# Two row tiles of x loaded from ScalarE's queue, the keys' weight second in SyncE's queue

## The chip, the cores and the metric

One core of a Trainium2 chip. The metric is the device time of one execution, in microseconds (us), lower is better. TensorE (PE) multiplies matrices, VectorE (DVE) and ScalarE (ACT) work elementwise, GpSimd (POOL) builds masks, and SyncE (SP) issues most transfers. ScalarE can issue transfers too, from a queue of its own. Both queues' transfers are carried by the core's 16 transfer engines.

## The reference

x has 2048 rows of 512, in bf16. Two blocks follow one another, each behind a layer norm without weights:

```python
h  = x + _A_ref(_layernorm(x), A_wqkv, A_wo)      # linear attention, 32 heads of 16
h2 = h + _B_ref(_layernorm(h), B_w1, B_w2)        # relu(.. @ w1) @ w2, inner width 1792

phi = lambda t: jnp.where(t > 0, t + 1, jnp.exp(t)) + 1e-6
pq, pk = phi(q), phi(k)
kv = einsum("bhsd,bhse->bhde", pk, v);  z = sum of pk over the rows
o  = (pq @ kv) / (pq . z + 1e-6)                  # then @ wo
```

## The kernel before

The rows are cut into 16 tiles of 128, and the tiles into four chunks of 512 rows. The order of all work is written out by hand: the string `ORDER` is a list of words, and each word calls the function `op_` of its name with the numbers behind it. The words are issued one after the other, each to the engine that its function names, so an engine works through its own words in the order of the string. Waits between engines and for transfers are put in for the data that a word reads and writes.

The words that matter here, t being a tile:

- `lx.t.n` loads n tiles of x from tile t on, issued by SP (line 219). `ax.t.n` does the same from ScalarE (line 222); the kernel before has the function and does not call it. `lk`, `lq`, `lv`, `lo`, `l1`, `l2` load weights (line 225); `lk` loads the keys' weight `wk_sb`, 512 KB.
- `table` loads the table of ScalarE's functions (line 183). `warm.n.b.w` issues n matmuls on zeros (line 250), ahead of the first real work of PE.
- `S.t` and `A.t` are the two steps of mean and variance of a tile of x (lines 253 and 254, VectorE). `R.t` makes 1/sqrt(var + eps) with a Ln and an Exp (lines 259 and 260, ScalarE). `N.t` normalises into `h_nat` (line 267, VectorE).
- `T.t` transposes the normalised tile on PE (line 292), `E.t` copies it out of PSUM on ScalarE (line 302). From tile 5 on most tiles are transposed by a transfer instead (`X.t`, line 313).
- `K.t` multiplies tile t by the keys' weight (line 321), `Q` projects queries (line 329), `G` accumulates (line 373). `F`, `U`, `M`, `D` make phi of the keys.
- In the second half `h.t` multiplies by the folded output weight (line 501), `hD.t` adds x on VectorE and so empties its bank (line 507), `s.t`, `a.t`, `n.t` are the second layer norm on VectorE (lines 255, 256, 275), `x.t` its transpose by transfer (line 314). `p` and `f` are the two matmuls of the feed-forward block (lines 516 and 545), `pD` and `fo` their evictions on VectorE (lines 536 and 553), and `fd` stores.

In the kernel before, all loads go through SP: tile 0, tile 1, tile 2, the keys' weight, tile 3, tiles 4 and 5, tiles 6 and 7, the queries' weight, and then four tiles at a time. On PE the first real words are T.0, T.1, T.2, K.0, K.1, T.3, K.2, K.3.

The table of the order is one string; no other function differs between the kernels.

Of the kernel before, what the change touches and what calls it, by code (L numbers as in the profile page):

```python
# [15 lines left out]


ORDER = """
table const lx.0.1 warm.66.7.64 lx.1.1 masks lx.2.1 lk.0.4 lx.3.1 S.0 lx.4.2 S.1 lx.6.2 lq.0.4 A.0 A.1 S.2 R.0.1
warm.2.7 lx.8.4 R.1.1 N.0 lx.12.4 A.2 N.1 T.0.1 R.2.1 T.1.6 E.0 N.2 E.1 T.2.4 S.3 K.0.2 E.2 A.3 S.4 K.1.4.2.2 R.3.1  # L20
K.1.4.0.2 F.0.1 N.3 A.4 U.0.1 S.5 T.3.5 K.2.6.2.2 E.3 S.7 K.2.6.0.2 F.1.1 K.3.3.0.2 M.0.1 A.5 U.1.1 D.0.1 K.3.3.2.2
M.1.1 R.4.2 Q.0.3.1 S.6 F.3.1 A.7 A.6 N.5 F.2.1 Q.0.1.5 N.4 X.5 R.6.2 D.1.1 T.4.7 U.3.1 M.2.1 Q.0.0.4 M.3.1 S.8 E.4
lo.0.2 U.2.1 S.10 Q.0.2.0 qF.0.0.2 N.6 K.4.2 N.7 X.6 A.10 A.8 qU.0.0.2 S.9 K.5.3 D.3.1 X.7 A.9 D.2.1 R.8.2 G.0 S.15
F.4.2 N.8 G.1 S.13 X.8 U.4.2 S.14 G.3 qU.0.2.2 A.13 S.12 lv.0.2 G.2 M.4.2 A.12 N.9 K.7.3 R.12.2 A.15 D.4.2 X.9
qF.0.2.2 K.6.2 N.12 A.14 S.11 R.14.2 X.12 K.8.0 F.6.2 N.15 N.14 G.4 A.11 N.13 U.6.2 M.6.2 X.13 qM.0.0.2 K.9.1 R.10.2
qD.0.0.2 K.12.2 X.15 D.6.2 U.8.2 za.4.1 G.5 F.8.2 X.14 K.13.3 N.11 N.10 za.6.0 G.6 X.11 U.12.2 G.7 M.8.2 F.12.2 X.10
qM.0.2.2 K.14.0 D.8.2 M.12.2 K.15.1 lv.2.2 za.8.0 l1.0.2 K.11.3 l1.2.2 F.14.2 D.12.2 K.10.2 zf U.14.2 qD.0.2.2 G.9 zhi
F.10.2 M.14.2 G.13 zlo U.10.2 G.8 M.10.2 D.14.2 G.12 D.10.2 z.0.0 z.2.0 z.3.0 z.1.0 G.15 zc zh d4.0.2 G.11 dl4.0 dx4.0
G.14 wb.0 G.10 lo.2.2 Q.1.1.1 gA.2.2 gD.0.2 rb.0.4 Q.1.0.0 ab.0.1 rb.0.6 ab.0.3 kv.1.7 rb.0.2 kv.3.7 ab.0.7 kv.0.7
rb.0.0 kv.2.7 ab.0.5 Q.1.3.3 l2.7.7 kx qF.1.0.2 Q.1.2.2 qU.1.0.2 qM.1.0.2 m.0.4 m.2.6 m.1.5 qF.1.2.2 qD.1.0.2 m.3.7  # L30
Q.2.0.0 mD.0.2 mA.2.2 Q.2.1.1 qU.1.2.2 dm.0.0.2 Q.2.3.7 dm.0.2.2 qF.2.0.2 h.1.6 qM.1.2.2 qD.1.2.2 qU.2.0.2 h.0.2 hD.1
d4.1.4 s.1 Q.3.1.5 a.1 hD.0 nA.1 h.3.0 s.0 dl4.1 x.1 h.2.2 a.0 hD.3 nA.0 Q.2.2.6 s.3 dx4.1 x.0 Q.3.2.0 a.3 hD.2
qF.2.2.2 n.3 wb.1 Q.3.3.1 s.2 qU.2.2.2 x.3 Q.3.0.4 a.2 n.2 qF.3.2.2 qM.2.0.2 x.2 qM.2.2.2 ph.0.3.3.0 qU.3.2.2 qD.2.2.2
ph.0.0.6.0 ph.0.1.7.0 qM.3.2.2 rb.1.7 qU.3.0.2 ph.0.2.2.0 qD.3.2.2 rb.1.3 ph.0.11.1.0 rb.1.5 qD.2.0.2 ph.0.10.0.0
qF.3.0.2 rb.1.6 ph.0.10.0.1 rb.1.1 ph.0.11.1.1 rb.1.0 p.0.5.4 pD.0.10.2 rb.1.4 rb.1.2 ph.0.2.2.1 ph.0.3.3.1 l2.0.7
qM.3.0.2 ph.0.0.6.1 pD.0.2.2 p.0.6.0 ph.0.1.7.1 qD.3.0.2 p.0.4.3 pD.0.0.2 p.0.7.1 pA.0.4.2 dm.1.2.2 d4.2.5.2 dm.1.0.2
p.0.8.2 dl4.2 pD.0.6.2 dl4.3 p.0.9.3 dx4.2 p.0.13.5 dx4.3 pD.0.8.2 wb.2 r.0.4 h.4.7 h.6.0 hD.4 rb.2.3 f.3.1.0.7 rb.2.1
s.4 rb.2.0 a.4 rb.2.6 rb.2.2 p.0.12.4 rb.2.5 rb.2.7 h.7.2 pD.0.12.2 rb.2.4 f.3.1.7.7 wb.3 hD.7 s.7 h.5.4 hD.6
f.2.3.7.7 hD.5 f.1.6.0.7 dm.2.2.2 dm.2.0.2 s.6 rb.3.2 h.8.0 rb.3.7 a.6 s.5 f.1.6.7.7 rb.3.0 hD.8 rb.3.5 rb.3.6 n.4 s.8
rb.3.3 f.2.3.0.7 a.5 rb.3.1 fo.1 rb.3.4 n.5 a.7 x.5 h.9.7 n.7 n.6 fo.2 f.0.0.7.7 x.4 fo.3 dm.3.2.2 h.10.5 x.7 dm.3.0.2  # L40
h.11.6 hD.9 x.6 hD.10 h.13.3 s.10 h.15.2 fd.3.0.2 fd.3.2.2 a.10 a.8 n.10 hD.11 h.14.7 x.10 s.11 f.0.0.0.7 n.8 a.11
hD.15 s.9 p.1.3.5 hD.13 p.1.8.2 hD.14 fo.0 p.1.2.4 s.15 h.12.1 s.14 p.1.9.3 s.13 a.13 p.1.7.7 pD.1.8.2 p.1.6.6 a.9
n.11 r.8.4 n.13 p.1.12.0 n.9 r.4.4 a.14 a.15 x.9 n.14 p.1.11.3 hD.12 pD.1.2.2 p.1.13.1 x.11 p.1.10.2 n.15 pD.1.6.2 x.8
p.1.0.5 pD.1.10.2 p.1.5.4 fd.1.0.2 fd.1.2.2 x.14 p.1.1.6 s.12 pD.1.12.2 f.5.2.7.7 fd.2.0.2 fd.2.2.2 fd.0.0.2 fd.0.2.2
x.15 pD.1.0.2 p.1.4.3 p.2.2.5 pD.1.4.2 f.5.2.0.7 p.2.6.3 fo.5 p.2.7.4 p.2.3.6 pD.2.6.2 p.2.10.1 a.12 n.12 r.12.4
p.2.4.4 pD.2.2.2 x.12 f.7.0.0.7 fd.5.0.2 fd.5.2.2 x.13 f.7.0.7.7 p.2.5.5 fo.7 p.2.11.2 pD.2.4.2 p.2.12.3 pD.2.10.2
p.2.13.4 f.4.6.0.7 pD.2.12.2 p.2.0.5 p.3.2.1 p.3.3.2 f.4.6.7.7 f.6.0.0.7 fo.4 pD.3.2.2 p.3.9.7 p.3.8.6 f.6.0.7.7
pD.3.8.2 p.2.9.1 fo.6 p.2.1.6 fd.6 p.3.1.3 p.3.0.2 p.2.8.0 pD.3.0.2 p.3.11.4 pD.2.0.2 p.3.10.3 pD.2.8.2 p.3.5.2
# [550 lines left out]
```

## Time and profile before

| | |
|---|---|
| median of 3 runs | 168.88 us (168.74 to 168.93) |
| profiled execution | 168.48 us, span 166.8 us |
| PE | busy 162.6 us, 98% of the span |
| VectorE | busy 115.9 us, 69% |
| ScalarE | busy 49.5 us, 30% |
| HBM read, written | 9.96 MB, 2.62 MB |
| mean granted TensorE clock | 0.999 |

The profiled execution is one execution; its span runs from the first instruction to the last, and its own time lies 1.68 us above the span. Times in the views count from the span's start. In a timeline, a row gives the start, the length, the engine, the line, what is written from what, how many instructions are merged, and in brackets how long the engine had been idle before and what ended it. "SPq" and "ACTq" are the transfer issues of SyncE and ScalarE: the length is that of the issue, not of the transfer.

### The profile page before, as it was taken

How to read it: one execution, taken by the hardware profiler on the slowest of the kernel's cores; microseconds unless marked ns; L12 is line 12 of the kernel's file. 1: busy time of each engine (PE TensorE's matmuls, PEld its weight loads, DVE VectorE, ACT ScalarE, POOL GpSimd, SP SyncE). 2: the span in 40 equal slices, each digit the busy share in tenths (PEclk: the TensorE clock that was granted, in tenths of full speed). 3: DMA queues.
4: the chain of work that ended last, by engine and by line, in shares of the span. 5: the costliest groups of instructions: out<-in, count | busy, mean ns of one | idle time of the engine just before them, and what ended most of it. 6: DMA issues, size and time to landing. Idle time of an engine off the chain costs nothing.

```text
span 166.8 us, 2421 instructions
## 1 busy us (share of the span) xinstructions
PE 162.6 (98%) x920; PEld 79.8 (48%) x920; DVE 115.9 (69%) x215; ACT 49.5 (30%) x83; POOL 4.8 (3%) x21
## 2 busy tenths in 40 slices
PE   7999999999999999999999999999999999999993
PEld 7544444454544774444444444444444444464442
DVE  3899999942599979668999899564535484400532
ACT  3899996715777916200000020010000000000000
POOL 7400000000000000000000000000000000000000
PEclk9999999999999999999999999999999999999999
DMA  4975555763752446231352035312000000020122
GB/s 113 346 300 126 125 97 103 276 253 96 170 177 51 111 135 210 72 94 56 111 109 69 0 63 93 100 30 64 0 0 4 31 0 0 7 97 2 44 95 73
DMA packets 26811, 16.28 MB, mean 98 GB/s; under 512 B 16176, under 2 KB 25776, under 8 KB 26800
## 3 DMA queue, kind: packets, MB, share of 16 engines
q1 hardware_dynamic: 26336, 15.84, 33.9%
q10 hardware_dynamic: 464, 0.30, 0.7%
q8 instruction: 7, 0.11, 0.3%
q14 instruction: 4, 0.03, 0.1%
HBM read 9.96 MB, written 2.62 MB: 75 GB/s over the span
## 4 chain that ended last, share of the span: by engine, by line
PE 94%; DVE 2%; DMA 1%; ACT 0%; issue 0%
PE bk L545 29%; PE bk L516 26%; PE bk L321 8%; PE bk L373 8%; PE bk L329 8%; PE bk L501 8%; PE bk L525 3%; DMA x_nat<-in_A_x_dram 1%; DVE st L253 1%; PE bk L445 1%; DVE gT L553 1%; PE bk L397 1%; PE bk L292 1%; PE bk L419 1%; PE bk L431 1%; DVE h_nat L267 0%
## 5 line engine op out<-in xcount | busy, mean ns | idle before, releaser
L545 PE MATMUL bk<-w_sb,at 128*128 128x512 bf16 (+2 forms) x252 | 50.9, 355 | 0.0
L516 PE MATMUL bk<-lnT,w_sb 128*128 128x512 bf16 x200 | 45.6, 379 | 0.0
L536 DVE TENSOR_SCALAR at<-bk 128x1024 bf16<-128x1024 f32 x27 | 32.4, 1220 | 13.6 <-PE bk L516 10.6
L545 PEld LDWEIGHTS <-at 128*128 128x128 bf16 x252 | 23.5, 98 | 25.2 <-DVE at L536 0.3
L516 PEld LDWEIGHTS <-w_sb 128*128 128x128 bf16 x200 | 19.5, 98 | 23.1 <-issue 0.4
L553 DVE SCALAR_TENSOR_TENSOR gT<-bk,rstd,h_nat 128x512 bf16<-128x512 f32 (+2 forms) x18 | 12.1, 688 | 22.6 <-PE bk L545 20.2
L339 ACT ACTIVATE eb<-bk 128x1024 bf16<-128x1024 f32 (+1 forms) x18 | 16.6, 930 | 3.5 <-PE bk L419 1.6
L259 ACT ACTIVATE rstd<-mv,eps 128x2 f32<-128x2 f32 (+2 forms) x14 | 4.1, 294 | 44.4 <-DVE mv L256 41.6
L342 ACT ACTIVATE rb<-bk 128x1024 bf16<-128x1024 f32 (+1 forms) x18 | 16.6, 936 | 0.9 <-PE bk L321 0.9
L501 PE MATMUL bk<-m_sb,pqs 128*128 128x512 bf16 x64 | 15.3, 379 | 0.0
L321 PE MATMUL bk<-wk_sb,lnT 128*128 128x512 bf16 x64 | 15.1, 379 | 0.0
L329 PE MATMUL bk<-lnT,wq_sb 128*128 128x512 bf16 x64 | 15.0, 379 | 0.0
L373 PE MATMUL bk<-at,h_nat 128*128 128x512 bf16 x56 | 13.2, 379 | 0.0
L253 DVE BATCH_NORM_STATS2 st<-x_nat 128x6 f32<-128x512 bf16 x16 | 10.5, 675 | 1.9 <-DMA x_nat<-in_A_x_dram 1.9
L507 DVE TENSOR_TENSOR h_nat<-bk,x_nat 128x512 bf16<-128x512 f32 x16 | 10.7, 679 | 0.9 <-PE bk L501 0.8
L255 DVE BATCH_NORM_STATS2 st<-h_nat 128x6 f32<-128x512 bf16 x16 | 10.8, 687 | 0.2
L501 PEld LDWEIGHTS <-pqs 128*128 128x128 bf16 x64 | 6.3, 98 | 7.6
L373 PEld LDWEIGHTS <-h_nat 128*128 128x128 bf16 x64 | 6.1, 98 | 7.3 <-issue 0.2
L321 PEld LDWEIGHTS <-lnT 128*128 128x128 bf16 x64 | 6.0, 97 | 7.4 <-ACT lnT L302 0.3
L329 PEld LDWEIGHTS <-wq_sb 128*128 128x128 bf16 x64 | 6.1, 98 | 7.1 <-issue 0.2
L346 DVE TENSOR_SCALAR eb<-eb 128x1024 bf16<-128x1024 bf16 (+1 forms) x18 | 6.7, 389 | 0.3 <-ACT eb L339 0.3
L267 DVE TENSOR_SCALAR h_nat<-x_nat,mv,rstd 128x512 bf16<-128x512 bf16 x16 | 6.1, 400 | 0.3 <-ACT rstd L260 0.3
(62 smaller groups left out, 90.8 us busy)
## 6 DMA issues: line engine op xcount, KB each, us to landing
w_sb<-in_B_w_dram SPq DMA_DIRECT2D x4, 896.0 KB, 5.0
rr<-scr SPq DMA_DIRECT2D x28, 64.0 KB, 2.6
out_dram<-gT SPq DMA_DIRECT2D x10, 128.0 KB, 1.9
x_nat<-in_A_x_dram SPq DMA_DIRECT2D x2, 512.0 KB, 7.1
out_dram<-gT SPq DMA_DIRECT2D x11, 64.0 KB, 1.6
x_nat<-in_A_x_dram SPq DMA_DIRECT2D x4, 128.0 KB, 2.2
wk_sb<-in_A_wqkv_dram SPq DMA_DIRECT2D x1, 512.0 KB, 4.2
x_nat<-in_A_x_dram SPq DMA_DIRECT2D x2, 256.0 KB, 4.5
```

What stands on the lines that cost most here:

```text
L253: op_S = lambda t: nc.vector.bn_stats(out=st[:, t, :], in_=x_nat[:, t, :])
L255: op_s = lambda t: nc.vector.bn_stats(out=st2[:, t, :], in_=h_nat[:, t, :])
L321: nc.tensor.matmul(bk[:, b, :], lhsT=lnT[c][:, kd, j * P : (j + 1) * P], rhs=wk_sb[:, kd, :], **part(("k", t), KD),)
L329: nc.tensor.matmul(bk[:, b, :], lhsT=wq_sb[:, kd, j * P : (j + 1) * P], rhs=lnT[c][:, kd, :], start=(kd == 0), stop=(kd == KD - 1),)
L339: nc.scalar.activation(out=buf(eb, kind, i, n), in_=bank(at_bank[kind, i], n), func=ACT.Exp)
L342: nc.scalar.activation(out=buf(rb, kind, i, n), in_=bank(at_bank[kind, i], n), func=ACT.Relu)
L373: nc.tensor.matmul(bk[:, KD + kd, :], lhsT=ln_nat[:, t, kd * P : (kd + 1) * P], rhs=pk(t)[:, 0, :], start=(not stated), stop=(len(stated) ...
L501: nc.tensor.matmul(bk[:, b, :], lhsT=pqs[:, (c * KD + jb) % NQ, j * P : (j + 1) * P], rhs=m_sb[:, jb, :], start=(jb == 0), stop=(jb == KD ...
L516: nc.tensor.matmul(bk[:, b, :], lhsT=w1_sb[:, kd, f * P : (f + 1) * P], rhs=lnT[c][:, kd, :], start=(kd == 0), stop=(kd == KD - 1),)
L536: nc.vector.tensor_scalar(out=acts[c % 2][:, f : f + n, :], in0=bank(at_bank["p", c, f], n), scalar1=-1.0, scalar2=0.0, op0=ALU.mult, op1= ...
L545: nc.tensor.matmul(bk[:, b, 0 : w * P], lhsT=acts[c % 2][:, f, j * P : (j + 1) * P], rhs=w2_sb[:, f, k * P : (k + w) * P], **part(("f", t, ...
L553: nc.vector.scalar_tensor_tensor(out=o_t[:, t % NO, cols], in0=bk[:, at_bank["f", t, k], 0 : w * P], scalar=rstd2[:, t : t + 1], in1=h_nat ...
```

## The change

Tiles 1 and 2 of x are loaded with `ax` by ScalarE, ahead of its table load; so SP issues the keys' weight directly behind tile 0. The first words of `ORDER`:

```diff
-table const lx.0.1 warm.66.7.64 lx.1.1 masks lx.2.1 lk.0.4 lx.3.1 S.0 lx.4.2 S.1 lx.6.2 lq.0.4 A.0 A.1 S.2 R.0.1
+ax.1.1 const lx.0.1 warm.66.7.64 ax.2.1 lk.0.4 masks table lx.3.1 lx.4.2 lx.6.2 S.0 lq.0.4 lx.8.4 S.1 lx.12.4 A.0 A.1
...
```

The functions called are these, as they stand in both kernels:

```python
def op_lx(t, n):
    nc.sync.dma_start(out=x_nat[:, t : t + n, :], in_=rows_of(xf, t, n))

def op_ax(t, n):
    nc.scalar.dma_start(out=x_nat[:, t : t + n, :], in_=rows_of(xf, t, n))
```

SyncE at the program's start, before. `x_nat` is x in SBUF, `wk_sb` the keys' and `wq_sb` the queries' weight:

```order
L594 UNCONDITIONAL_BRANCH
L219 DMA x_nat<-in_A_x_dram 128x512 x3
L225 DMA wk_sb<-in_A_wqkv_dram 128x4x512
L219 DMA x_nat<-in_A_x_dram 128x512
L219 DMA x_nat<-in_A_x_dram 128x1024 x2
L225 DMA wq_sb<-in_A_wqkv_dram 128x4x512
```

The same place after the change:

```order
L594 UNCONDITIONAL_BRANCH
L219 DMA x_nat<-in_A_x_dram 128x512
L225 DMA wk_sb<-in_A_wqkv_dram 128x4x512
L219 DMA x_nat<-in_A_x_dram 128x512
L219 DMA x_nat<-in_A_x_dram 128x1024 x2
L225 DMA wq_sb<-in_A_wqkv_dram 128x4x512
```

Two of the three single tiles ahead of the keys' weight are gone from SP's queue; all behind them keeps its order and moves up by two places.

They stand on ScalarE now. Its start, as the difference of the two orders:

```order
 L594 UNCONDITIONAL_BRANCH
+L222 DMA x_nat<-in_A_x_dram 128x512 x2
 L183 ACT_TABLE_LOAD
 L259 ACTIVATE rstd<-mv,eps_77 128x1
```

Two issues have come in front of the table load and of all of ScalarE's activations. The orders of PE and of GpSimd are the same as before, and that of VectorE is the same up to the second half.

There VectorE moves two steps of the second layer norm, between the evictions of the feed-forward block (`at` is its inner activation, `gT` holds the output tiles):

```order
 L507 TENSOR_TENSOR h_nat<-bk,x_nat 128x512
-L255 BN_STATS st_106<-h_nat 128x6
+L255 BN_STATS st_106<-h_nat 128x6 x2
 L507 TENSOR_TENSOR h_nat<-bk,x_nat 128x512 x2
 L553 SCALAR_TENSOR_TENSOR gT<-bk,rstd_108,h_nat 128x512
-L255 BN_STATS st_106<-h_nat 128x6 x3
+L255 BN_STATS st_106<-h_nat 128x6 x2
 L256 BN_AGGR mv_107<-st_106 128x2
 L536 TENSOR_SCALAR at_101<-bk 128x1024
```

The statistics of tile 15 (s.15) stand ahead of the evictions hD.13 and hD.14 and of the output eviction fo.0. A little later n.14 moves behind s.12, past hD.12, n.15 and three evictions `pD`. In `ORDER` many other words change their places beside words of other engines, which moves nothing on any one engine.

More of the change, by code (lines that the diff above doesn't have):

```diff
@@ L18 @@
 ORDER = """
-table const lx.0.1 warm.66.7.64 lx.1.1 masks lx.2.1 lk.0.4 lx.3.1 S.0 lx.4.2 S.1 lx.6.2 lq.0.4 A.0 A.1 S.2 R.0.1
[L20 to L43, printed above, removed]
@@ L44 @@
-p.1.0.5 pD.1.10.2 p.1.5.4 fd.1.0.2 fd.1.2.2 x.14 p.1.1.6 s.12 pD.1.12.2 f.5.2.7.7 fd.2.0.2 fd.2.2.2 fd.0.0.2 fd.0.2.2
-x.15 pD.1.0.2 p.1.4.3 p.2.2.5 pD.1.4.2 f.5.2.0.7 p.2.6.3 fo.5 p.2.7.4 p.2.3.6 pD.2.6.2 p.2.10.1 a.12 n.12 r.12.4
+ax.1.1 const lx.0.1 warm.66.7.64 ax.2.1 lk.0.4 masks table lx.3.1 lx.4.2 lx.6.2 S.0 lq.0.4 lx.8.4 S.1 lx.12.4 A.0 A.1
+warm.2.7 S.2 R.0.1 R.1.1 N.0 A.2 N.1 T.0.1 R.2.1 T.1.6 E.0 N.2 S.3 E.1 T.2.4 K.0.2 E.2 A.3 S.4 R.3.1 K.1.4.2.2 F.0.1
+N.3 K.1.4.0.2 A.4 U.0.1 S.5 T.3.5 K.2.6.2.2 E.3 S.7 K.2.6.0.2 F.1.1 K.3.3.0.2 M.0.1 A.5 U.1.1 D.0.1 K.3.3.2.2 M.1.1
@@ new lines @@
+R.4.2 S.6 Q.0.3.1 F.3.1 A.7 A.6 N.5 F.2.1 Q.0.1.5 N.4 X.5 R.6.2 D.1.1 T.4.7 U.3.1 M.2.1 Q.0.0.4 M.3.1 S.8 E.4 lo.0.2
+U.2.1 S.10 Q.0.2.0 qF.0.0.2 N.6 N.7 K.4.2 X.6 A.10 A.8 qU.0.0.2 S.9 K.5.3 D.3.1 X.7 A.9 D.2.1 R.8.2 G.0 S.15 F.4.2 N.8
+G.1 S.13 X.8 U.4.2 S.14 G.3 qU.0.2.2 A.13 S.12 lv.0.2 G.2 M.4.2 A.12 N.9 K.7.3 R.12.2 A.15 D.4.2 X.9 qF.0.2.2 K.6.2
+N.12 A.14 S.11 R.14.2 X.12 K.8.0 F.6.2 N.15 N.14 G.4 A.11 N.13 U.6.2 M.6.2 X.13 qM.0.0.2 K.9.1 R.10.2 qD.0.0.2 K.12.2
+X.15 D.6.2 U.8.2 za.4.1 G.5 F.8.2 X.14 K.13.3 N.11 N.10 za.6.0 G.6 X.11 U.12.2 G.7 M.8.2 F.12.2 X.10 qM.0.2.2 K.14.0
@@ new lines @@
+D.8.2 M.12.2 K.15.1 lv.2.2 za.8.0 l1.0.2 K.11.3 l1.2.2 F.14.2 D.12.2 K.10.2 zf U.14.2 qD.0.2.2 G.9 zhi F.10.2 M.14.2
+G.13 zlo U.10.2 G.8 M.10.2 D.14.2 G.12 D.10.2 z.0.0 z.2.0 z.3.0 z.1.0 G.15 zc zh d4.0.2 G.11 dl4.0 dx4.0 G.14 wb.0
+G.10 lo.2.2 Q.1.1.1 gA.2.2 gD.0.2 rb.0.4 Q.1.0.0 ab.0.1 rb.0.6 ab.0.3 rb.0.2 kv.1.7 kv.3.7 ab.0.7 rb.0.0 kv.0.7 kv.2.7
+ab.0.5 l2.7.7 Q.1.3.3 kx qF.1.0.2 Q.1.2.2 qU.1.0.2 qM.1.0.2 m.0.4 m.2.6 m.1.5 qF.1.2.2 qD.1.0.2 m.3.7 Q.2.0.0 mD.0.2
+mA.2.2 Q.2.1.1 qU.1.2.2 dm.0.0.2 Q.2.3.7 dm.0.2.2 qF.2.0.2 h.1.6 qM.1.2.2 qD.1.2.2 qU.2.0.2 h.0.2 hD.1 d4.1.4 s.1
@@ new lines @@
+Q.3.1.5 a.1 hD.0 nA.1 h.3.0 s.0 dl4.1 x.1 h.2.2 a.0 hD.3 nA.0 Q.2.2.6 s.3 dx4.1 x.0 Q.3.2.0 a.3 hD.2 qF.2.2.2 n.3 wb.1
+Q.3.3.1 s.2 qU.2.2.2 x.3 Q.3.0.4 a.2 n.2 qF.3.2.2 qM.2.0.2 x.2 qM.2.2.2 ph.0.3.3.0 qU.3.2.2 qD.2.2.2 ph.0.0.6.0
+ph.0.1.7.0 qM.3.2.2 rb.1.7 qU.3.0.2 ph.0.2.2.0 qD.3.2.2 rb.1.3 ph.0.11.1.0 rb.1.5 qD.2.0.2 ph.0.10.0.0 qF.3.0.2 rb.1.6
+ph.0.10.0.1 rb.1.1 ph.0.11.1.1 rb.1.0 p.0.5.4 pD.0.10.2 rb.1.4 rb.1.2 ph.0.2.2.1 ph.0.3.3.1 l2.0.7 qM.3.0.2 ph.0.0.6.1
+pD.0.2.2 p.0.6.0 ph.0.1.7.1 qD.3.0.2 p.0.4.3 pD.0.0.2 p.0.7.1 pA.0.4.2 dm.1.2.2 d4.2.5.2 dm.1.0.2 p.0.8.2 dl4.2
@@ new lines @@
+pD.0.6.2 dl4.3 p.0.9.3 dx4.2 p.0.13.5 dx4.3 pD.0.8.2 wb.2 r.0.4 h.4.7 h.6.0 hD.4 rb.2.3 rb.2.1 f.3.1.0.7 s.4 rb.2.0
+a.4 rb.2.6 rb.2.2 p.0.12.4 rb.2.5 rb.2.7 h.7.2 pD.0.12.2 rb.2.4 wb.3 f.3.1.7.7 hD.7 s.7 h.5.4 hD.6 f.2.3.7.7 hD.5
+dm.2.2.2 f.1.6.0.7 dm.2.0.2 s.6 rb.3.2 rb.3.7 a.6 s.5 h.8.0 rb.3.0 rb.3.5 f.1.6.7.7 hD.8 rb.3.6 rb.3.3 n.4 s.8 rb.3.1
+f.2.3.0.7 a.5 rb.3.4 fo.1 n.5 a.7 x.5 n.7 h.9.7 n.6 fo.2 f.0.0.7.7 x.4 fo.3 dm.3.2.2 x.7 dm.3.0.2 h.10.5 hD.9 h.11.6
+hD.10 x.6 h.13.3 s.10 fd.3.0.2 fd.3.2.2 a.10 h.15.2 a.8 n.10 hD.11 x.10 h.14.7 s.11 f.0.0.0.7 n.8 a.11 hD.15 s.9
@@ L46 @@
+p.1.3.5 s.15 hD.13 p.1.8.2 hD.14 p.1.2.4 fo.0 s.14 h.12.1 s.13 p.1.9.3 a.13 p.1.7.7 pD.1.8.2 p.1.6.6 a.9 n.11 r.8.4
+n.13 p.1.12.0 n.9 r.4.4 a.14 a.15 x.9 hD.12 p.1.11.3 pD.1.2.2 p.1.13.1 x.11 n.15 p.1.10.2 pD.1.6.2 x.8 p.1.0.5
+pD.1.10.2 p.1.5.4 fd.1.0.2 fd.1.2.2 s.12 p.1.1.6 n.14 pD.1.12.2 x.14 f.5.2.7.7 pD.1.0.2 fd.2.0.2 fd.2.2.2 p.1.4.3
+fd.0.0.2 fd.0.2.2 x.15 p.2.2.5 pD.1.4.2 f.5.2.0.7 p.2.6.3 fo.5 p.2.7.4 p.2.3.6 pD.2.6.2 p.2.10.1 a.12 n.12 r.12.4
 p.2.4.4 pD.2.2.2 x.12 f.7.0.0.7 fd.5.0.2 fd.5.2.2 x.13 f.7.0.7.7 p.2.5.5 fo.7 p.2.11.2 pD.2.4.2 p.2.12.3 pD.2.10.2
```

## The prediction

> **What bounds the kernel now.** I read the page first, then the chain of waits from the span's start, then the timeline of each engine in the first 9 us, then the transfers. The page:
>
> ```profile
> PE 162.6 (98%) x920; PEld 79.8 (48%) x920; DVE 115.9 (69%) x215; ACT 49.5 (30%) x83; POOL 4.8 (3%) x21
> PE 94%; DVE 2%; DMA 1%; ACT 0%; issue 0%
> ```
>
> TensorE (PE) is busy for 98% of the span and carries 94% of the chain. What is left is the start, up to the first projection matmul, and the last store. The chain of waits, in order of time (start, us, what):
>
> ```profile
> 0.80 2.05 DMA x_nat<-in_A_x_dram
> 2.85 0.02 issue
> 2.87 1.30 DVE st L253 x2
> 4.18 0.14 DVE mv L254 x2
> 4.32 0.65 DVE st L253
> ...
> 5.97 0.42 DVE h_nat L267
> 6.40 0.05 issue
> 6.44 0.40 PE bk L292 x4
> 6.84 1.88 PE bk L321 x8
> 8.72 0.30 PE bk L292 x4
> 9.02 1.73 PE bk L321 x8
> ...
> 12.47 0.22 PE bk L292 x4
> ```
>
> Tile 0 of x lands at 0.80 + 2.05 = 2.85. From there VectorE (DVE) runs S.0, S.1, A.0, A.1, S.2, N.0, A.2, N.1, N.2, and the chain stays with these steps and the rstd of tile 2. N.2 ends at 6.39, PE transposes tile 2 at 6.44 (T.2), and behind that transpose, in PE's own order, stands K.0, the first key projection. From there the chain is PE alone, piece on piece. So what the start gains or loses goes one for one into the time, and the start hangs on the landing of tile 0, not on the keys' weight. Which instructions waited for a transfer in this stretch, from the timelines of VectorE and of ScalarE (ACT):
>
> ```profile
> 2.87 1.30 DVE L253 BATCH_NORM_STATS2 st<-x_nat 128x6 f32<-128x512 bf16 x2 [1.63 <-DMA x_nat<-in_A_x_dram]
> 6.64 0.69 DVE L253 BATCH_NORM_STATS2 st<-x_nat 128x6 f32<-128x512 bf16 x1 [0.26 <-DMA x_nat<-in_A_x_dram]
> 0.80 1.28 ACT L183 ACT_TABLE_LOAD   x1 [0.80 <-PEq L583]
> 4.29 0.30 ACT L259 ACTIVATE rstd<-mv,eps 128x1 f32<-128x1 f32 x1 [2.21 <-DVE mv L254]
> ```
>
> Two waits only: S.0 for tile 0, and S.3 for tile 3. S.1 and S.2 do not wait: tiles 1 and 2, which the change sends from another queue, are early enough already.
>
> **The change part by part.** The sum is made on the profiled execution: 168.48 us, its span 166.8 and 1.68 around it. The median of the runs is 168.88, 0.40 above, and I carry that difference over. About 0.2%, 0.34 us, is what a measurement of this kernel can tell from no change.
>
> The issues now, from the timeline of SyncE's queue (SP), and their landings from the lists of transfers: tile 0; tile 1, whose row tile 2 repeats; the keys' weight.
>
> ```profile
> 0.80 1.34 SPq L219 DMA_DIRECT2D x_nat<-in_A_x_dram  x3
> 2.18 0.43 SPq L225 DMA_DIRECT2D wk_sb<-in_A_wqkv_dram  x1
> 2.66 1.45 SPq L219 DMA_DIRECT2D x_nat<-in_A_x_dram  x3
> x_nat<-in_A_x_dram SPq DMA_DIRECT2D x1, 128.0 KB, 2.0
> x_nat<-in_A_x_dram SPq DMA_DIRECT2D x1, 128.0 KB, 2.2
> wk_sb<-in_A_wqkv_dram SPq DMA_DIRECT2D x1, 512.0 KB, 4.2
> ```
>
> One issue takes 1.34 / 3 = 0.45 us. Tiles 0, 1 and 2 go out at 0.80, 1.25 and 1.70 and land at 2.85, 3.45 and 3.9; the keys' weight goes out at 2.18 and lands at 6.38. After the change tile 1 goes out at 0.80 from ScalarE, beside tile 0, and tile 2 at 1.25, beside the keys' weight; what follows on SP goes out 2.18 - 1.25 = 0.93 earlier.
>
> *Tile 0* is the term that decides. Now tile 1 is issued 0.45 behind it in the same queue; afterwards tile 1 stands beside it from the first byte. The transfers' rate in four stretches (last two columns: DMA share, GB/s):
>
> ```profile
> 1.80:2.40 0.60, 0.60 (x16) 0.60 (x14) 0.00 (x0) 0.28 (x1) 0.53 (x3) 1.00 0.80 224
> 3.60:4.40 0.80, 0.80 (x19) 0.80 (x17) 0.80 (x4) 0.11 (x1) 0.68 (x3) 1.00 0.86 116
> 4.40:5.40 1.00, 1.00 (x10) 0.36 (x7) 1.00 (x4) 0.78 (x4) 0.81 (x4) 1.00 1.05 365
> 5.40:5.80 0.40, 0.40 (x5) 0.40 (x5) 0.29 (x1) 0.36 (x2) 0.35 (x2) 1.00 1.12 394
> ```
>
> From 1.8 to 2.4 the engines are 80% busy and move 0.6 x 224 = 134 KB, as much as tile 0 has (131 KB). It cannot land earlier than now: it is issued at the same 0.80 and is first in its queue. The low end of its delay: both tiles at the best rate of these rows, 262 KB at 394 GB/s, take 0.67 us instead of 0.6, +0.07. The high end: the rate stays, and tile 0 is through when tile 1 is now, at 3.45, +0.6. The nearest rows are from the one place where both queues issue together, the spreads into rr at 40.56 (SP's, then ScalarE's), against the first of a burst that SP issues alone at 57.18:
>
> ```profile
> rr<-scr SPq DMA_DIRECT2D x1, 64.0 KB, 3.0
> rr<-scr ACTq DMA_DIRECT2D x1, 64.0 KB, 3.3
> rr<-scr SPq DMA_DIRECT2D x1, 64.0 KB, 2.6
> ```
>
> Beside one of ScalarE's, SP's transfer takes 3.0 us instead of 2.6, +0.4. That lies between the ends and I take it: S.0 at 3.27, and the chain up to K.0 0.40 later.
>
> The Trainium skill, "DMA: Bandwidth & Descriptors", section "Issuing engines are not separate DMA queues", speaks against the change: transfers started by different engines run on the same 16 DMA engines and interleave, and a second issuer saves only issue time. By that rule with no gain in rate, tile 0 would end with tile 1 and the sum would have +0.6 where I have +0.4; the rr rows, 3.0 and 3.3, agree with the interleaving.
>
> *Tile 1*: in the rr pair ScalarE's transfer lands 0.3 behind SP's, so about 3.55; S.1 needs it after S.0, at 3.27 + 0.65 = 3.92. Nothing; that 0.37 is its cover. *Tile 2*: S.2 needs it at 4.32 + 0.40 = 4.72. Tiles 0, 1, 2 and as much of the weight again are 524 KB; at 250 GB/s, an estimate between the first and third of the rates above, they are through at 3.9, and with the 0.45 that tile 0 has from its last byte (2.4) to its landing, at 4.35. In time: 0. The ends are 0 and the weight's own landing, 1.25 + 4.2 = 5.45, 0.73 late.
>
> *The table load* now follows two issues on ScalarE: it starts at 0.80 + 2 x 0.45 = 1.70 and ends at 2.98. Its cover is the wait for A.0: the first activation comes at 4.29, after the change at 4.69. Nothing.
>
> *The keys' weight* goes out 0.93 earlier, but K.0 stands behind T.2 on PE (6.44 now), later than the weight's present 6.38. Nothing. *Tile 3* goes out at 1.73 instead of 2.66, and S.3's wait of 0.26 goes. On PE there are two holes that it could close: T.3 takes 0.30 at 8.72 where T.4 takes 0.22 at 12.47 (0.08), and the K piece before it 1.88 where the next takes 1.73 (0.15). But N.3 also waits for its rstd on ScalarE, which stands behind three evictions:
>
> ```profile
> 6.07 1.57 ACT L302 ACTIVATE lnT<-bk 128x512 bf16<-128x512 bf16 x3
> 7.59 0.30 ACT L259 ACTIVATE rstd<-mv,eps 128x1 f32<-128x1 f32 x1
> ```
>
> These move with the start, so rstd of tile 3 is what is late next. I take -0.05; the ends are 0 and -0.23.
>
> *The late reorder on VectorE*: s.15 goes ahead of hD.13, hD.14 and fo.0; n.14 goes behind s.12.
>
> ```profile
> 90.39 1.27 DVE L507 TENSOR_TENSOR h_nat<-bk,x_nat 128x512 bf16<-128x512 f32 x2
> 93.71 8.80 PE L516 MATMUL bk<-lnT,w_sb 128*128 128x512 bf16 x40
> 128.25 9.66 PE L516 MATMUL bk<-lnT,w_sb 128*128 128x512 bf16 x44
> ```
>
> One bn_stats, 0.65, puts the end of the two evictions from 91.66 to 92.3; p.1.9, which takes the bank of hD.13, is not before 93.71. Chunk 3, which n.14 feeds, begins after 128. Nothing; without that cover 0.65.
>
> Sum: +0.40 - 0.05 = +0.35. Profiled 168.83, median 169.23.
>
> **The rivals.** *B, tile 2 is caught behind the weight's beginning.* For it: from 3.6 to 4.4, where the weight begins now, the rate is 116 GB/s, against 365 after it. If that slump comes with the weight it now falls on tile 2: 0.8 x (1 - 116 / 365) = 0.55 us lost, 4.35 becomes 4.90, 0.18 late; towards the end of 0.73 if tile 2 waits in line. I price it at +0.35, which gives 169.58. It decides if tile 2 lands after S.1's end. Against it: tile 2 is in a queue of its own.
>
> *C, tile 0 is not disturbed*, because the second queue fills the 20% that the engines are idle, or because ScalarE's transfer begins late (its 0.3 in the rr pair). Then the change does nothing that counts: tile 0 at 2.85 to 2.95, and -0.05 from T.3, up to -0.23 if both holes close: 168.65 to 168.95, 168.85 in the middle, not slower. It decides if tile 0 lands by 3.0.
>
> *D, PE slows down again.* T.0 now follows the warming matmuls without a pause (they end at 5.40, N.0 at 5.29); 0.40 later PE stands idle for about 0.3 us before it. A wide matmul takes, among the warming ones and later:
>
> ```profile
> L250 PE MATMUL bk<-m_sb 128*128 128x512 bf16 x2 | 1.0, 624 | 0.0
> L321 PE MATMUL bk<-wk_sb,lnT 128*128 128x512 bf16 x64 | 15.1, 379 | 0.0
> ```
>
> If the pause put off the change from the first to the second, the first eight K matmuls would cost 8 x 0.245 = 2.0 more: 171.2. Against it: a pause of 0.3 in over four busy us. *E, faster* by over 0.34 needs more than both holes (0.23) and tile 0 as now; I see no work that would give it.
>
> **How the numbers follow.** My forecast A (tile 0 later by 0.2 to 0.6) 0.52, B 0.20, C 0.18, D 0.04, E 0.06. A's +0.35 lies at the bound of 0.34, so half of A counts as slower and half as no change. Slower: 0.26 + 0.20 + 0.04 = 0.50; the same: 0.26 + 0.18 = 0.44; faster: 0.06. The range: below, C's end, 168.65; above, A's sum with tile 2 at its worst, 169.23 + 0.73 = 169.96, so 170.0. D and most of E are left out.
>
> **What would show it.** Right: S.0 starts at about 3.3 with a wait of some 2.0 for its transfer, tile 1's landing close behind, no wait at S.1, S.2 and S.3, T.2 at about 6.8 and PE's pieces the same length from there on. Wrong: S.0 still at 2.87 (C); a wait of S.2 for x_nat (B); wide K matmuls of over 600 ns (D); or a difference that arises after 10 us, where I expect none.

## The result and the profile after

The changed kernel takes 170.68 us (median of 14 runs, 169.39 to 171.46); the kernel before took 168.77 beside it (14 runs, 168.50 to 169.52). The ratio is 1.0098, with an interval of 1.0074 to 1.0122: slower by 1.65 us, by the ratio. The forecast was 169.23 with a range up to 170.0. Two things stand out: the loss is about five times what I forecast, and the changed kernel's runs lie 2 us apart where those of before lie within about 1.

The profile shown is of one of the quickest executions, 169.41 us with a span of 167.7. The page, as before:

```profile
PE 162.3 (97%) x920; PEld 79.7 (48%) x920; DVE 115.6 (69%) x215; ACT 49.4 (29%) x83; POOL 4.7 (3%) x21
```

The chain of waits from the start:

```profile
0.80 2.80 DMA x_nat<-in_A_x_dram
3.60 0.02 issue
3.62 1.29 DVE st L253 x2
...
7.10 0.42 DVE h_nat L267
7.52 0.05 issue
7.57 0.40 PE bk L292 x4
7.96 1.73 PE bk L321 x8
9.69 0.22 PE bk L292 x4
9.91 1.73 PE bk L321 x8
```

Tile 0 lands at 3.60 instead of 2.85, and T.2 starts at 7.57 instead of 6.44, 1.13 later. The two small holes are closed, as 1.73 and 0.22 show. Of the 1.13, tile 0 makes 3.60 - 2.85 = 0.75. VectorE's timeline and PE's tell where the other 0.38 arose, and what else is new:

```profile
3.62 1.29 DVE L253 BATCH_NORM_STATS2 st<-x_nat 128x6 f32<-128x512 bf16 x2 [2.38 <-DMA x_nat<-in_A_x_dram]
5.40 0.69 DVE L253 BATCH_NORM_STATS2 st<-x_nat 128x6 f32<-128x512 bf16 x1 [0.27 <-DMA x_nat<-in_A_x_dram]
...
1.05 4.28 PE L250 MATMUL bk<-m_sb 128*128 128x64 bf16 x68 [1.05 <-DVE m_sb L191]
6.46 0.78 PE L292 MATMUL bk<-ident,h_nat 128*128 128x128 bf16 x8 [1.14 <-DVE h_nat L267]
```

S.2, which waited for nothing before, now waits for tile 2. And PE stands idle for 1.14 us before T.0. Before, its warming matmuls reached up to T.0, as PE's timeline of the kernel before shows:

```profile
1.05 4.56 PE L250 MATMUL bk<-m_sb 128*128 128x64 bf16 x68 [1.05 <-DVE m_sb L191]
5.40 0.86 PE L292 MATMUL bk<-ident,h_nat 128*128 128x128 bf16 x8
6.44 0.40 PE L292 MATMUL bk<-ident,h_nat 128*128 128x128 bf16 x4 [0.19 <-DVE h_nat L267]
6.72 2.00 PE L321 MATMUL bk<-wk_sb,lnT 128*128 128x512 bf16 x8
```

For this pair of profiles the account closes: 0.75 from tile 0, 0.38 from S.2 on (0.27 of it the wait for tile 2), less 0.23 from the two holes, is 0.90, and the spans differ by 167.7 - 166.8 = 0.9. It does not tell why the other executions take up to 2 us more.

### The profile page after: what moved, and what is told of

The parts are those of the page before. It is cut to its first block, busy times and chain, and to the rows that moved or that the text cites. A ratio compares the mean times of both kernels' runs of the same rounds, so it can differ in the third digit from the quotient of the medians.

```text
span 167.7 us, 2419 instructions
## 1 busy us (share of the span) xinstructions
PE 162.3 (97%) x920; PEld 79.7 (48%) x920; DVE 115.6 (69%) x215; ACT 49.4 (29%) x83; POOL 4.7 (3%) x21
## 4 chain that ended last, share of the span: by engine, by line
PE 93%; DVE 2%; DMA 2%; ACT 1%; issue 0%
PE bk L545 28%; PE bk L516 26%; PE bk L373 8%; PE bk L329 8%; PE bk L501 8%; PE bk L321 8%; PE bk L525 3%; DMA x_nat<-in_A_x_dram 2%; DVE st L253 1%; PE bk L445 1%; DVE gT L553 1%; PE bk L397 1%; PE bk L419 1%; PE bk L431 1%; PE bk L292 1%; DVE h_nat L267 0%
```

## The experiments

The times of each are set against the kernel before, run beside it on the same chip (medians 168.75 to 168.96).

**More warming matmuls, and fewer.** First the changed kernel:

```diff
-warm.66.7.64
+warm.90.7.64
```

> The changed kernel with 90 narrow warming matmuls instead of 66, so that PE has work for 24 x 0.053 = 1.3 us more, up to about the time that T.0 comes (6.46 in the profile after). Theory P (the pause): the first transposes and projections come 1.1 us later because tiles 0 and 2 land later, and what lies above that, and the wide spread of the changed kernel's runs (169.39 to 171.46), is PE's clock, which the pause of 1.1 us before T.0 lets open late or close again. Then all runs lie at 169.4 to 169.9, within 0.5 us of one another. Theory L (landings alone): the landings themselves differ from run to run by up to 2 us; then the runs keep their spread from 169.4 to 171.4 and the median stays near 170.7.

Four runs: 170.45, 170.49, 170.53, 171.33, ratio 1.0109 (1.0067 to 1.0151). The level is not the 169.4 to 169.9 of theory P; it is near theory L's 170.7, but three of the four runs lie within 0.1 us, without L's spread. The profile (170.49) shows one cause in PE's timeline:

```profile
7.72 1.89 PE L321 MATMUL bk<-wk_sb,lnT 128*128 128x512 bf16 x8
...
32.64 1.04 PE L321 MATMUL bk<-wk_sb,lnT 128*128 128x512 bf16 x4 [1.00 <-DMA lnT<-h_nat]
```

The start is that of the changed kernel at full speed, but a transpose by transfer came late at 32.6 and cost 1.0. Whether the other three runs had that too is not known, so this run does not decide between the theories.

Then the kernel before, with a pause of about the same length and the old loads:

```diff
-warm.66.7.64
+warm.42.7.64
```

> The kernel before with 42 narrow warming matmuls instead of 66: the loads are as before, but PE pauses for about 1.3 us ahead of T.0 at 5.4. Theory P: the runs spread and rise by 0 to 2 us, to between 168.8 and 170.8, with T.0 and K.0 starting where they did (5.4 and 6.7). Theory L: 168.8 as before, at most 0.2 off.

Measured 171.09 (169.92 to 171.32, 6 runs), ratio 1.0109 (1.0074 to 1.0143). PE's timeline:

```profile
5.34 1.71 PE L292 MATMUL bk<-ident,h_nat 128*128 128x128 bf16 x12 [1.02 <-DVE h_nat L267]
6.87 2.79 PE L321 MATMUL bk<-wk_sb,lnT 128*128 128x512 bf16 x8
```

T.0 starts where it did, at 5.34, after a pause of 1.02, and the eight K matmuls take 2.79 instead of the 2.00 of the kernel before and the 1.89 of the changed kernel. T.3 starts at 9.50 instead of 8.62. With the landings as before, fewer warming matmuls and the pause they leave cost 0.9 us in this execution. The profile also has two late transposes, 0.49 and 0.80 us, which make most of the rest of its 2.5 us over the profile of before. Theory L falls, and four of the six runs lie above the upper end of theory P's range. The granted clock does not show the slow start: it reads 1.00 in each us from 5 to 13, while the K matmuls run at half speed. The row from 7 to 8:

```profile
7.00:8.00 1.00, 1.00 (x4) 0.30 (x2) 0.76 (x2) 0.67 (x2) 0.00 (x0) 1.00 0.98 321
```

**A tiny transfer from ScalarE in the kernel before.**

```diff
-table const lx.0.1
+tx.16 table const lx.0.1
```

> The kernel before with one tiny transfer (16 pieces of 8 bytes of x, into a tile that nothing reads) issued by ScalarE ahead of its table load; all loads stay on SP. It tells why tile 0 landed at 3.60 instead of 2.85 after the change. Theory Q (the second queue's beginning): the transfer engines crawl for about half a us when ScalarE's queue starts beside SP's (36 GB/s from 2.0 to 2.2 in the profile after), whatever it carries; then tile 0 lands at about 3.3 to 3.5 here, and the time is up by 0.5 us or more. Theory S (sharing of bytes, the prediction's): with 128 bytes beside it tile 0 lands at 2.85 to 2.95 and the time is 168.8 as before.

Measured 169.07 (168.57 to 169.92), ratio 1.0008 (0.9987 to 1.0029). VectorE's S.0:

```profile
2.87 1.29 DVE L253 BATCH_NORM_STATS2 st<-x_nat 128x6 f32<-128x512 bf16 x2 [1.62 <-DMA x_nat<-in_A_x_dram]
```

Tile 0 is as early as before. A second queue in use, with 128 bytes on it, costs nothing that can be measured; theory Q falls.

**The late order alone**, on the loads of before (the words `ax` and `table` put back as they were).

> The loads as in the kernel before, the rest of the order as in the changed kernel: it has VectorE's late moves (s.15, n.14) alone. The prediction gave them nothing: 168.6 to 169.0. If they cost, the time is above 169.2 with the start as before.

Measured 169.11 (168.45 to 169.89), ratio 1.0006 (0.9984 to 1.0028). The late moves cost nothing that can be measured.

**The changed kernel again, twice**, for more profiles.

> The changed kernel once more, for a profile of another of its executions; its times spread from 169.39 to 171.46. Theory P (the pause of 1.1 us before T.0): an execution above 170.3 shows the wide matmuls of the K stage at 0.43 us apart for a while, as the kernel before with fewer warming matmuls did until 8.65. Theory H (late transposes): in such an execution the K stage starts at full speed and PE waits once, for 0.4 to 1.2 us, for a transpose by transfer (lnT) later on, as the runs with more warming matmuls (1.0 at 32.6) and with the late order (0.3 at 23.4) did.

> As the run before it, for a second profile of the changed kernel. Theory P: matmuls at 0.43 us apart at the start of the K stage. Theory H: a late lnT in the profile of each execution above 170.3, and full speed at the K stage's start.

The first gave runs of 171.90, 171.11 and 169.93; the profile is of the 171.90. Its VectorE, its PE, and the granted clock (the third column from the end, 1.00 for full speed) in three stretches:

```profile
3.27 1.29 DVE L253 BATCH_NORM_STATS2 st<-x_nat 128x6 f32<-128x512 bf16 x2 [2.02 <-DMA x_nat<-in_A_x_dram]
6.43 0.69 DVE L253 BATCH_NORM_STATS2 st<-x_nat 128x6 f32<-128x512 bf16 x1 [1.66 <-DMA x_nat<-in_A_x_dram]
...
7.50 0.78 PE L292 MATMUL bk<-ident,h_nat 128*128 128x128 bf16 x8 [2.41 <-DVE h_nat L267]
8.60 0.61 PE L292 MATMUL bk<-ident,h_nat 128*128 128x128 bf16 x4 [0.32 <-DVE h_nat L267]
9.00 3.23 PE L321 MATMUL bk<-wk_sb,lnT 128*128 128x512 bf16 x8
...
7.00:8.00 1.00, 0.50 (x6) 0.34 (x7) 0.83 (x4) 0.40 (x2) 0.00 (x0) 1.00 1.09 366
8.00:9.00 1.00, 0.68 (x9) 0.51 (x7) 0.87 (x2) 1.00 (x3) 0.00 (x0) 0.64 1.10 391
9.00:10.00 1.00, 1.00 (x5) 0.45 (x4) 0.90 (x3) 0.83 (x3) 0.00 (x0) 0.50 1.03 410
```

Tile 0 is earlier here (3.27) than in the first profile, and yet the run is 2.5 us longer: S.2 waits 1.66 us for tile 2, PE pauses for 2.41, and then the clock is at half, so that the K piece takes 3.23. T.2 is 1.03 later than in the first profile (8.60 against 7.57); the clock makes the other 1.5. The second run's profile is of a 169.79: tile 2 at 5.67, a pause of 1.58, full speed in the K stage. No late lnT stands behind either: theory H falls for the first, and P holds for it; the second is too quick to test either. Tile 2's landing is what sets the pause. In the runs of the result, five of the fourteen have a mean granted clock of 0.99, and they are all above 170.8, with a mean of 171.20; the others have 1.00, lie at 169.39 to 170.79 and have a mean of 170.02. So the clock is not the whole spread. Of the six runs here, 171.90 and 171.59 have 0.99, but 171.11 and 170.83 have 1.00; no profile shows what these two waited for, and a slow start like that of the run with fewer warming matmuls would not show in the mean clock.

**Tile 1 issued later from ScalarE.**

```diff
-ax.1.1 const lx.0.1
+tx.16 ax.1.1 const lx.0.1
```

> The changed kernel with a tiny transfer ahead of tile 1 on ScalarE, so that tile 1 is issued at 1.22 instead of 0.80 and tile 2 at 1.65; SP's queue is as after the change. Theory B (the two big transfers that begin together get in each other's way at their start, where the engines moved 26 to 82 GB/s from 1.8 to 2.4): tile 0 lands at 2.85 to 3.0 again, tile 1 by 3.7; K.0 at 7.2 or earlier, the time down by 0.4 to 0.7 us from the changed kernel. Theory S (sharing of bytes in flight): tile 0 still lands at 3.3 or later, since tile 1 and the keys' weight stand beside it, and the time is the changed kernel's.

Measured 172.79 (171.96 to 173.28, 4 runs), ratio 1.0236 (1.0201 to 1.0271), the worst of all. Tile 0 behaves as theory B has it, but tile 1 takes the place of tile 2, and the time goes the other way than B had it. VectorE, and the landings of tile 1 and of the weight (in us from the issue at 1.24 and 1.26):

```profile
3.00 0.69 DVE L253 BATCH_NORM_STATS2 st<-x_nat 128x6 f32<-128x512 bf16 x1 [1.76 <-DMA x_nat<-in_A_x_dram]
5.99 0.69 DVE L253 BATCH_NORM_STATS2 st<-x_nat 128x6 f32<-128x512 bf16 x1 [2.30 <-DMA x_nat<-in_A_x_dram]
...
x_nat<-in_A_x_dram ACTq DMA_DIRECT2D x1, 128.0 KB, 4.7
wk_sb<-in_A_wqkv_dram SPq DMA_DIRECT2D x1, 512.0 KB, 4.8
```

S.0 starts at 3.00, so tile 0 lost time to what begins with it, not to what stands beside it later. But tile 1, 128 KB, now lands with the 512 KB of the weight. PE pauses for 2.98 us before T.0, and its granted clock is 0.50 from 8 to 11; K.0 starts at 9.35. The packets of the two queues (q1 is SP's, q10 ScalarE's; packets, MB, share of the engines) from 2.4 to 3.2, from 3.2 to 4.0 and from 4.0 to 5.0:

```profile
q1 hardware_dynamic: 96, 0.08, 65.0%
q10 hardware_dynamic: 7, 0.00, 0.5%
...
q1 hardware_dynamic: 79, 0.08, 44.2%
q10 hardware_dynamic: 2, 0.00, 0.7%
...
q1 hardware_dynamic: 245, 0.25, 70.4%
q10 hardware_dynamic: 135, 0.12, 35.8%
```

In the slow beginning of the weight SP's queue moves 175 packets, 0.16 MB, in 1.6 us (the last of tile 0 among them), and ScalarE's queue moves 9. Only after it do both move.

**Half of the change**: tile 2 back on SP, ahead of the weight.

```diff
-ax.2.1 lk.0.4
+lx.2.1 lk.0.4
```

> Half of the change: tile 1 from ScalarE, tile 2 on SP again, ahead of the keys' weight. It takes out what tile 2 paid for standing beside the weight (it landed at 5.38, 0.47 after S.1's end at 4.91). Expected: tile 0 lands at 3.5 to 3.7 as after the change, tile 2 by 4.5, S.2 does not wait; K.0 at 7.3 to 7.5 instead of 7.80, the time 0.3 to 0.5 below the changed kernel's. If tile 2 is as late as before, it is not the weight that holds it up.

Measured 169.31 (168.63 to 170.11, 10 runs), ratio 1.0036 (1.0018 to 1.0055), 0.6 us. That is 1.05 us below the changed kernel by the ratios, more than the 0.3 to 0.5 expected; the mean granted clock is 1.00 in all ten runs. VectorE and PE:

```profile
3.30 1.29 DVE L253 BATCH_NORM_STATS2 st<-x_nat 128x6 f32<-128x512 bf16 x2 [2.07 <-DMA x_nat<-in_A_x_dram]
4.72 0.66 DVE L253 BATCH_NORM_STATS2 st<-x_nat 128x6 f32<-128x512 bf16 x1
...
7.09 1.24 PE L321 MATMUL bk<-wk_sb,lnT 128*128 128x512 bf16 x5
...
9.33 0.40 PE L292 MATMUL bk<-ident,h_nat 128*128 128x128 bf16 x4 [0.35 <-DVE h_nat L267]
```

S.2 waits for nothing. Tile 0 is 0.43 later than before, earlier than the 3.5 to 3.7 expected, and K.0 0.37 later (7.09 against 6.72). T.3 then waits 0.35 for N.3: tile 3, behind the weight, lands at 7.33 here, 0.7 later than before. T.3 starts 0.71 later, so about half of what this profile loses up to there comes from tile 3.

**Wide warming matmuls in the changed kernel.**

```diff
-warm.2.7 S.2
+warm.7.7 S.2
```

> The changed kernel with five more wide warming matmuls (7 instead of 2), which keep PE busy to 6.1 to 7.0 us whichever way its clock stands. The landings stay late. Theory: the slowest executions of the changed kernel (171.9 in the profile where PE idled for 2.4 us before T.0 and ran its K stage at half speed up to 11.9) owe some 1.5 us of it to the clock, the rest to tile 2. Then the runs here lie at 169.4 to 170.6, none above 171, and the profile shows matmuls 0.216 apart from K.0 on. If the clock has no part in the spread, the runs reach 171.4 again.

Measured 169.85 (169.36 to 170.59, 10 runs), ratio 1.0063 (1.0042 to 1.0085), the runs as expected but for one 0.04 below. All ten have a mean granted clock of 1.00. The profile has S.2 at 5.96 after 1.04 of waiting, so tile 2 is as late as ever, but PE goes on at full speed:

```profile
1.05 5.13 PE L250 MATMUL bk<-m_sb 128*128 128x64 bf16 x72 [1.05 <-DVE m_sb L191]
7.03 0.79 PE L292 MATMUL bk<-ident,h_nat 128*128 128x128 bf16 x8 [0.84 <-DVE h_nat L267]
8.12 0.40 PE L292 MATMUL bk<-ident,h_nat 128*128 128x128 bf16 x4 [0.32 <-DVE h_nat L267]
8.36 1.89 PE L321 MATMUL bk<-wk_sb,lnT 128*128 128x512 bf16 x8
```

**The weight behind tile 3 in SP's queue.** In the order SP then reads `lx.0.1`, `lx.3.1`, `lk.0.4`:

```diff
-ax.2.1 lk.0.4 masks table lx.3.1 lx.4.2
+ax.2.1 masks table lx.3.1 lk.0.4 lx.4.2
```

> The changed kernel with the keys' weight behind tile 3 in SP's queue, so that tile 2 on ScalarE stands beside tile 3 (128 KB) instead of the weight (512 KB). If tile 2 was late because it lands about when the big transfer beside it does (5.38 to 6.41 beside a weight that lands at 5.9 to 6.2), it now lands by 4.6, tile 3 with it, and the time is near that of the version with tile 2 on SP, 169.1 to 169.6. If it is ScalarE's second transfer as such that is slow, tile 2 still lands after 5.2 and the time stays at 170 and more.

Measured 169.20 (median of 10), the ratio 1.0008 (0.9992 to 1.0025). Eight runs lie at 168.92 to 169.53 and two at 171.5. The ratio is that of the eight; with all ten, the mean is 0.45% above the kernel before. The profile is of one of the two, which have a mean granted clock of 0.99. VectorE, PE and the granted clock from 9 to 10:

```profile
4.90 0.66 DVE L253 BATCH_NORM_STATS2 st<-x_nat 128x6 f32<-128x512 bf16 x1
...
8.34 3.42 PE L321 MATMUL bk<-wk_sb,lnT 128*128 128x512 bf16 x8 [0.85 <-ACT rstd L259]
...
9.00:10.00 1.00, 1.00 (x3) 0.29 (x2) 0.98 (x3) 0.00 (x0) 0.00 (x0) 0.50 1.05 399
```

Even here S.2 does not wait for tile 2, which landed 3.0 after its issue at 1.24. In this execution it is the weight that comes late: issued at 1.72, it lands 6.6 later at 8.3, where K.0 starts, again at half the clock. (The view puts the wait down to a rstd that ends at 8.31, but K.0 reads the weight and tile 0's transpose, not that rstd.) It is the weight beside tile 2, not ScalarE's queue as such, that made it late; whether by its size or by its layout is not shown. No version tried beats the kernel before.

## Why the prediction was wrong

- **The bound was right.** In the profile of the 169.41 execution the time hangs on when PE can begin K.0, and after it PE is as dense as before. The late reorder costs nothing that can be measured (1.0006), and the table load, which ends at 3.01, stands before a first activation that waits for VectorE until 5.03. The earlier weight was costed at nothing because K.0 does not need it sooner; that it would stand in tile 2's way is the step below.
- **Tile 0, +0.40, had the right path, but its size was in part luck.** With tile 2 back on SP it landed 0.43 late and K.0 came 0.37 late. In the three profiles of the changed kernel it landed at 3.24, 3.52 and 3.60, so 0.39 to 0.75 late, which reaches beyond the high end of +0.6. The +0.4 was read from an rr pair beside which the 256 KB of `wo_sb` were still moving (issued at 39.15, 2.7 to its landing), and single rr transfers took 2.2 to 2.8 elsewhere, not always 2.6.
- **Tile 3, -0.05, had the right sign and was too small.** In the profiles of 169.41 and 169.79 both holes are closed, -0.23, the far end that I named. (With tile 2 on SP, tile 3 went out later, landed later than before, and T.3 waited for it.)
- **Tile 2, "in time: 0", is the step that failed.** I let the two queues take turns from the first byte and reckoned 4.35. It landed at 5.38, 5.67 and 6.41, near the weight (5.9 to 6.2): at the upper end of my bounds, the 5.45, and beyond. The row that should have decided was the slump to 116 GB/s where the weight begins. I had put it under rival B with 0.20; the packets of the run with tile 1 issued later show that ScalarE's queue all but stands while it lasts. In the first profile the wait and what follows it cost 0.38 us, against B's price of 0.35; in the two others S.2 waits longer, 0.65 and 1.66 instead of 0.27.
- **D, the clock, was the other miss.** I gave it 0.04, for a pause of 0.3 us, and treated it as a case beside B. But B makes D: with tile 2 late the pause is 1.1 to 2.4 us. It also came in another form than I had in mind, which was full speed put off: in the 171.90 execution T.0 and T.1 run at full speed (0.78 for eight) and the clock falls to half after them. That cost 1.5 us there, and five of the fourteen executions have the lower mean clock. D's 171.2 equals the mean of these five by coincidence, since it was made of tile 0 and another form of the slow clock, without tile 2. The cover that I named for PE, the warming matmuls up to 5.40, was costed for its presence and not for its loss.

What each part of the 1.65 us is worth is known roughly. The clock: with wide warming matmuls the ratio is 1.0063 instead of 1.0098, 0.6 us, and the five executions alone raise the mean by 5/14 of 1.18, 0.4 us. The weight's place: 1.0063 with the weight second and the clock open, against 1.0008 in the eight quick runs with the weight behind tile 3, is 0.55%, 0.9 us (the two versions also differ in five warming matmuls). What then remains for tile 0, with the holes closed, is 0.0008, 0.14 us, and +0.40 - 0.23 would be 0.17. The version with tile 2 on SP, 0.6 us, does not contradict that, since tile 3 is late in it. A difference of two such ratios has an interval of about 0.3%, 0.5 us, to either side: the weight's place is clear of it, the clock's share only just.

Open: why the weight's transfer begins so slowly and holds up the other queue. Neither was tried apart. Nor is it known what makes a transpose by transfer come late: four of the twelve profiles, each of another version, have such waits, of 0.2 to 1.0 us.

## What to carry to other kernels

A second queue does not make a small urgent load safe from a large one: beside the 512 KB weight, tile 2 landed about when the weight did, and ahead of it in the one queue it landed 1.5 to 2.5 us earlier (3.9). Issue what is needed first, alone, and keep large loads behind it. If PE is kept warm by filler work, size the filler for the latest start that the loads can cause, since a late load may be paid twice, once as the wait and once in clock. Here five more wide matmuls brought 1.0098 down to 1.0063; 24 more narrow ones showed no gain (1.0109, four runs).

## What the runs showed that I had not expected

After a pause of 2.41 us PE ran at half the clock for 3.4 us (granted 0.50 to 0.65 from 8.0 to 12.0), while after pauses of 1.14 and 1.58 it did not. The slow K matmuls after 44 warming matmuls and a pause of 1.02 are another case: there PE had not yet reached full speed, where here it had and lost it. The Trainium skill, "TensorE: Matmul & The Clock Gate", Part 1, has the gate judge PE's activity in free-running windows of about 3.4 us. The length agrees with the stretch at half clock here.

The moment at which PE first reaches full speed does differ between executions: in the three profiles of the changed kernel the clock rows kept with the traces put it at 4.92, 4.86 and 6.19, and the wide warming matmuls, which straddle it or come before it, take 466, 525 and 615 ns. But that does not explain the two sides: 4.92 (clock kept) and 4.86 (clock lost) nearly coincide, and what differs is the pause, 1.14 against 2.41. In the 3.41 us after that moment PE was busy for 1.00, 0.46 and 1.50 us in the three profiles that then fell to half clock (171.90, tile 1 later, weight third), and for 1.96 to 3.22 in the eight others that had reached full speed by 6.3. So in these profiles the bound lies between 1.50 and 1.96 us of 3.41; that it is the busy time in this stretch that decides, no run was made to show.

A tiny transfer on ScalarE's queue ahead of tile 1 brought tile 0 back to 2.98, since the two tiles no longer began together, and still made the slowest kernel of all.
